# Attention and gated-MLP kernel on one core: wider loads of keys, queries, values and gates, constant rows made on chip, and a new order of all steps

## Chip, cores and metric

One core of a Trainium2 chip runs the whole program. The metric is device time in microseconds (us) for one execution; lower is better. The engines are TensorE (PE; its weight loads appear as PEld), VectorE (DVE), ScalarE (ACT), GpSimd (POOL) and SyncE (SP), each with its own instruction stream. DMA transfers are issued from the streams of SP, ACT or POOL and all run on the same 16 DMA engines.

## What is computed

The reference is an mLSTM attention block followed by a gated MLP. Batch B=4, heads H=8, sequence S=768, head size D=40.

```
for t in range(S):
    m_new = max(f_gate[t] + m, i_gate[t])
    f_stab, i_stab = exp(f_gate[t] + m - m_new), exp(i_gate[t] - m_new)
    C = f_stab * C + i_stab * outer(v[t], k[t])
    n = f_stab * n + i_stab * k[t]
    y[t] = sigmoid(o_gate[t]) * (C @ q[t]) / max(|n . q[t]|, 1)
x = y with the heads side by side                 # (4, 768, 320)
h = relu(x @ w_in); u, v = halves of h            # 512 columns each
v_n = (v - mean) / sqrt(var + 1e-6)               # over the 512 columns
v_s = w_spatial @ v_n + b_spatial                 # over the 768 positions
out = (u * v_s) @ w_out
```

## The kernel before

**Attention** (function attention, from L557). The sequence is cut into chunks of 128 positions, six per batch, 24 in all, named by n; each chunk is two half-chunks of 64. For a chunk TensorE forms the scores of each head (step s, L605), the exponents of the decay matrix as one matrix product of two small tables, AT (positions) and GM (gates) (ex, L608), and in batch 0 also the decay of the queries (ebm, L618). ScalarE takes the exponential (W, L623), VectorE multiplies scores by it (ks, L629), GpSimd decays queries (q, L637) and keys (kt, L648). TensorE makes the state's increment (dc, L659/L661) and the outputs (pv, L702/L703); the state goes from chunk to chunk through the steps d1, c1, d2, c2 (L677 to L690). Then come the denominator (den, L714 to L717, three VectorE instructions), the division and the output gate (xm L720, xg L723), and a transposition (px, L743) that leaves x as a high and a low part (xh, xl).

**MLP.** a_v makes the v half and its normalisation (V, L796 and what follows), b_u the u half and the product with w_spatial (pu L856, pb L862 to L864), c_out the output (L899 to L901). Every operand of these products is split into a high and a low part, so each is three or two matrix products. The weights are split on chip: cvt (L442 to L490) for w_in and w_out with one ScalarE and several VectorE instructions, load_ws (L526 to L544) for w_spatial, whose low part is a VectorE subtraction at L540.

**Gates** (L320 to L431). The scans over 768 positions are cut into three pieces, z0 (128 positions), z1 (256) and z2 (384). z0's rows go straight from SBUF into GM (four small transfers on SP, steps dg, L418) and AT (two on ACT, da, L424). All pieces are also written to scratch arrays in memory (wg L404, wa L408, on the ACT stream; we L411, on SP), and later chunks read their rows from there (gm L584, ra L438; in batch 0 on the ACT stream, in later batches on SP; eb L592 on SP).

**Loads.** QK of a chunk is two transfers on SP of 40 partitions each (L572: partitions 64 to 103 and 0 to 39), from two buffers in turn. RH (values, keys and output gates) is two transfers of 64 partitions (L576), from three buffers in turn; GpSimd clears 32 partitions of each RH buffer once (L314). The constant rows of GM (84 partitions) and AT (68 partitions), two buffers each, come from memory by four transfers issued on GpSimd (L300, L303).

**Order.** The functions only register steps, each with an engine, the buffers that it reads and writes, and a cost. The order in which they are issued is a written-out list of names, ORDER (L98 to L150). The function ordered takes it as it is, and hands out buffer slots in that order; the costs and due times given to add decide nothing here. So every engine, and every DMA-issuing stream, runs its steps in the order of the list: a step that waits holds up all later steps of its stream. The list before begins:

```
half_neg rhz0 ident i sel f warm qk0_0 cgm0 qk0_1 cat0 rh0_0 cgm1 rh0_1 rhz1 wir_ld wi0 wi10_ld wi11_ld m0 rst rh1_0 m1 ksz2 rh1_1 ksz0 fa1 qk1_0 fs1
rhz2 qk1_1 fa0 ksz1 g1 s0 cat1 fs0 gh1 g0 eg1 is0 as0 gh0 gl1 ah0 dg0 gl0 da0 dg1 al0 wg1 m2 dg2 da1 dg3 wg0 eg0 fa2 th0 fs2 wa0 g2 gm1 ex0 is1 ebm0
```

Here qk, rh, cgm and cat are the loads named above; wir_ld, wi10_ld and wi11_ld load 512 KB of w_in each; m, fa, fs, g, is, as are the scans and subtractions of a piece, gh, gl, ah, al their high and low parts.

Of the kernel before, what the change touches and what calls it, by code (L numbers as in the profile page):

```python
# [98 lines left out]
half_neg rhz0 ident i sel f warm qk0_0 cgm0 qk0_1 cat0 rh0_0 cgm1 rh0_1 rhz1 wir_ld wi0 wi10_ld wi11_ld m0 rst rh1_0 m1 ksz2 rh1_1 ksz0 fa1 qk1_0 fs1  # L99
rhz2 qk1_1 fa0 ksz1 g1 s0 cat1 fs0 gh1 g0 eg1 is0 as0 gh0 gl1 ah0 dg0 gl0 da0 dg1 al0 wg1 m2 dg2 da1 dg3 wg0 eg0 fa2 th0 fs2 wa0 g2 gm1 ex0 is1 ebm0  # L100
gh2 rh2_0 W0 gl2 rh2_1 Eb0 as1 ks0_0 ebm1 wir_1 ks0_1 kt0 ah1 wir_2 we1 q0_1 Eb1 dc0 wir_3 wi10_1 c1_0 al1 wir_h0 qk2_0 wi10_2 pv0 qk2_1 is2 wa1 wir_4
wir_h1 den0 d2_0 wir_h2 wi10_3 wi11_1 xm0 as2 wir_h3 wi11_2 ra01 wi11_3 wi10_h0 wi10_4 wi11_h0 wir_s0 q1_0 ah2 wi11_4 gm2 wg2 xg0 q1_1 eg2 wir_5 ex1
rh3_0 th1 rh3_1 wi10_5 s1 W1 al2 wi10_s0 gm3 px0 qk3_0 wir_s1 kt1 wa2 qk3_1 ex2 wi11_5 xh0 we0 xj0 W2 wi11_s0 dc1 th2 wi10_l0 kt2 s2 ra02 wir_l1 ebm2
wi11_l0 Eb2 c2_0 dc2 gm4 xl0 d1_1 th3 xk0 ks1_0 V00 q2_0 ks1_1 c1_1 ks2_0 d2_1 pv1 ks2_1 re00 q2_1 c2_1 sq00 ex3 bsp den1 ebm3 s3 xm1 W3 d1_2 qk5_0
xg1 Eb3 qk5_1 va00 wir_l0 px1 kt3 rh4_0 gm5 rh4_1 c1_2 q3_0 xh1 dc3 ks3_0 xj1 ks3_1 pv2 d2_2 xl1 xk1 ex4 den2 q3_1 ebm4 W4 V01 c2_2 xm2 wi00_ld Eb4
xg2 wi01_ld d1_3 qk4_0 qk4_1 po00 px2 c1_3 re01 rh5_0 pv3 d2_3 nb00 rh5_1 xh2 xj2 ra10 xl2 gm6 th4 kt4 s5 c2_3 sq01 den3 we2 d1_4 xm3 ws00_ld dc4 vh00
# [867 lines left out]
```

## Time and profile before

| | |
|---|---|
| time, median of 3 runs | 421.42 us (419.78 to 424.54) |
| the profiled execution's own time | 424.52 us |
| its span, first to last instruction | 422.7 us |
| PE busy | 369.7 us, 87% of the span |
| DVE, ACT, POOL busy | 250.9, 152.5, 139.8 us |
| mean granted TensorE clock | 0.927 |
| bytes read and written in memory | 30.59 and 4.42 MB |

Starts are in us from the start of the span. In a row of a timeline the first number is the start, the second the length; in a row of waits the numbers are the total, the count and the longest; in a row of stages each engine's busy time stands with its count of instructions in brackets, and the three last columns are the granted TensorE clock, the mean busy share of the DMA engines and the rate in GB/s.

### The profile page before, as it was taken

The numbers are of one execution on the slowest core, as the hardware profiler recorded it, in microseconds if no ns is written. First come the engines' busy times: TensorE is split into PE (matmuls) and PEld (weight loads), VectorE is DVE, ScalarE is ACT, GpSimd is POOL, SyncE is SP. The second block draws the span as 40 slices with busy tenths as digits, with TensorE's granted clock in tenths as the row PEclk, the third lists the DMA queues.
The fourth block names the chain that finished last, engine by engine and source line by source line (L and its number), as shares of the span: only waits on it lengthen the run. The fifth ranks groups of instructions, "written<-read, shape, count | busy, mean of one in ns | idle before, by whom it ended". The sixth has DMA issues, their size and how long they took to land.

```text
span 422.7 us, 9190 instructions
## 1 busy us (share of the span) xinstructions
PE 369.7 (87%) x3654; PEld 335.1 (79%) x3654; DVE 250.9 (59%) x540; ACT 152.5 (36%) x363; POOL 139.8 (33%) x150
## 2 busy tenths in 40 slices
PE   2045996979969999989799989999799999999996
PEld 1023874768869998868699878998699998899995
DVE  6145979867998737569693574335952626434231
ACT  2044268646331205723501521156320408441212
POOL 8044578753350114546530313325440004230000
PEclk9999999677969999989779985999779999999999
DMA  9940569354820505326312073200210100000001
GB/s 166 227 116 12 133 202 223 118 139 118 213 75 18 158 30 143 102 79 154 101 46 73 7 185 92 85 16 24 72 47 2 33 16 2 33 16 2 16 33 47
DMA packets 17262, 35.62 MB, mean 84 GB/s; under 512 B 3960, under 2 KB 9196, under 8 KB 17220
## 3 DMA queue, kind: packets, MB, share of 16 engines
q1 hardware_dynamic: 12556, 29.72, 26.6%
q10 hardware_dynamic: 4136, 4.52, 3.3%
q0 software_dynamic: 528, 0.81, 1.2%
q8 instruction: 29, 0.48, 0.5%
q14 instruction: 13, 0.11, 0.1%
HBM read 30.59 MB, written 4.42 MB: 83 GB/s over the span
## 4 chain that ended last, share of the span: by engine, by line
PE 67%; DVE 14%; DMA 10%; issue 4%; ACT 3%; POOL 1%; SPq 1%; ACTq 0%; DVEq 0%; POOLq 0%
PE pu L856 9%; PE pb L862 8%; PE pb L863 8%; PE pb L864 8%; PE pm L796 7%; PE pv L702 5%; DMA QK<-in_qk 5%; PE s L605 5%; PE pv L703 4%; PE pc L899 3%; PE pc L901 3%; PE pc L900 2%; PE dc L659 2%; DMA RH<-in_vk 2%; DVE KS L629 2%
## 5 line engine op out<-in xcount | busy, mean ns | idle before, releaser
L637 POOL TENSOR_TENSOR KS<-QK,Eb 40x512 f32<-40x512 f32 x44 | 57.5, 1312 | 70.1 <-PE pv L703 32.8
L862 PE MATMUL pb<-wsH,vH 128*128 128x384 f32 x192 | 68.0, 354 | 3.9 <-DVE wo_r L468 3.9
L863 PE MATMUL pb<-wsL,vH 128*128 128x384 f32 x192 | 67.1, 350 | 0.0
L864 PE MATMUL pb<-wsH,vL 128*128 128x384 f32 x192 | 66.9, 349 | 0.0
L873 DVE TENSOR_TENSOR pb<-pb,bsp 128x384 f32<-128x384 f32 x32 | 18.1, 565 | 54.3 <-PE pb L864 54.3
L883 ACT CAST gt<-pb 128x384 fp32r<-128x384 f32 x32 | 15.4, 480 | 76.7 <-DVE pb L876 76.7
L703 PE MATMUL pv<-RH,KS 128*64 128x41 f32 x384 | 37.9, 254 | 5.1 <-DVE KS L629 3.2
L702 PE MATMUL pv<-RH,KS 104*64 104x41 f32 (+1 forms) x384 | 38.0, 253 | 4.7 <-DVE KS L629 3.0
L605 PE MATMUL s<-QK 40*64 40x64 f32 x768 | 34.3, 251 | 8.9 <-DMA QK<-in_qk 8.9
L862 PEld LDWEIGHTS pb<-wsH,vH 128*128 128x128 f32 x192 | 38.1, 198 | 4.4 <-DVE wo_r L468 4.2
L605 PEld LDWEIGHTS s<-QK 40*64 40x64 f32 x768 | 30.6, 162 | 13.5 <-DMA QK<-in_qk 9.2
L812 POOL TENSOR_TENSOR st<-st,half_neg 128x1 f32<-128x1 f32 x24 | 13.4, 560 | 82.0 <-DVE st L809 65.8
L702 PEld LDWEIGHTS pv<-RH,KS 104*64 104x64 f32 (+1 forms) x384 | 31.2, 158 | 10.9 <-POOL st L812 3.3
L836 POOL TENSOR_TENSOR vL<-v,vH 128x512 fp32r<-128x512 f32 x24 | 31.1, 1299 | 23.6 <-ACT vH L818 15.2
L863 PEld LDWEIGHTS pb<-wsL,vH 128*128 128x128 f32 x192 | 38.2, 199 | 0.0
L864 PEld LDWEIGHTS pb<-wsH,vL 128*128 128x128 f32 x192 | 38.0, 198 | 0.0
L703 PEld LDWEIGHTS pv<-RH,KS 128*64 128x64 f32 x384 | 31.2, 159 | 7.7 <-DVE KS L629 2.8
L629 DVE TENSOR_TENSOR KS<-s,W 64x512 f32<-64x512 f32 x48 | 32.9, 686 | 6.9 <-PE s L605 4.3
L648 POOL TENSOR_TENSOR RH<-RH,W 128x320 f32<-128x320 f32 x24 | 18.7, 781 | 49.0 <-ACT W L623 34.9
L856 PE MATMUL pu<-xH,wiH 128*128 128x384 f32 x96 | 33.1, 345 | 0.0
L856 PE MATMUL pu<-xH,wiL 128*128 128x384 f32 x96 | 32.6, 340 | 0.0
L796 PE MATMUL pm<-wiH,xH 128*128 128x512 f32 x72 | 31.5, 437 | 0.0
(117 smaller groups left out, 818.8 us busy)
## 6 DMA issues: line engine op xcount, KB each, us to landing
RH<-in_vk SPq DMA_DIRECT2D x48, 242.0 KB
QK<-in_qk SPq DMA_DIRECT2D x48, 160.0 KB
out<-o ACTq DMA_DIRECT2D x24, 160.0 KB
Eb<-scr_e SPq DMA_DIRECT2D x33, 80.0 KB
ws<-in_w_sp SPq DMA_DIRECT2D x12, 192.0 KB
wi_raw<-in_w_in SPq DMA_DIRECT2D x4, 512.0 KB
wo_raw<-in_w_out SPq DMA_DIRECT2D x4, 320.0 KB
wir_raw<-in_w_rem SPq DMA_DIRECT2D x1, 512.0 KB
```

Source lines behind the costliest of these rows:

```text
L605: self.nc.tensor.matmul(o[64 - p0:128 - p0, h], q[p0:p0 + D, 0, h], q[p0:p0 + D, 1, h], start=True, stop=True)
L629: self.nc.vector.tensor_tensor(out=KS.t[r, e], in0=st()[r], in1=self.T(W)[r], op=ALU.mult)
L637: self.nc.gpsimd.tensor_tensor(out=KS.t[r, e], in0=self.T(QK)[r, 1], in1=self.T(Eb)[r], op=ALU.mult)
L648: self.nc.gpsimd.tensor_tensor(out=kt, in0=kt, in1=self.T(W)[:, :, L - 1:L].broadcast_to([128, H, D]), op=ALU.mult)
L702: self.nc.tensor.matmul(o[0:64, h], ks[0:ke, 0, h], v0[0:ke, h], start=True, stop=True)
L703: self.nc.tensor.matmul(o[64:128, h], ks[:, 1, h], v1[:, h], start=True, stop=True)
L796: self.nc.tensor.matmul(pmt(), l, r, start=i == 0, stop=i == len(terms) - 1)
L836: self.nc.gpsimd.tensor_tensor(out=vl(), in0=vt(), in1=vh().bitcast(F32), op=ALU.subtract)
L856: self.nc.tensor.matmul(put(), w, x, start=i == 0, stop=i == len(terms) - 1)
L862: self.nc.tensor.matmul(pbt(), vH[:, cd], wh[:, s], start=s == 0, stop=False)
L863: self.nc.tensor.matmul(pbt(), vH[:, cd], wl[:, s], start=False, stop=False)
L864: self.nc.tensor.matmul(pbt(), vL[:, cd], wh[:, s], start=False, stop=s == NB - 1)
```

## The change

Keys and queries of a chunk come in one transfer of 112 partitions; the rows between are zeros laid into the input (448 KB in place of two of 160 KB). Values of the second half-chunk, keys and gates come in one transfer of 128 partitions (484 KB, zeros included, which replaces the clearing by GpSimd), values of the first half-chunk in another of 64 partitions (82 KB). Of the constant rows only a few come from memory: a 64 by 64 mask (16 KB), 16 rows for each GM (32 KB) and 4 for each AT (12 KB); the other rows are copied on chip from the mask and from the identity matrix, by ScalarE for the first buffer and GpSimd for the second. In the gates, the additions and subtractions of z1 and z2 that ran on VectorE go to GpSimd, and the scratch writes and the reads of batch 0 go from the ACT stream to SP. The low parts of the first half of w_spatial go from VectorE to GpSimd. In batch 0 the denominator is one ScalarE and two VectorE instructions in place of three on VectorE. The two products of each head in pv change places. ORDER is new throughout. Costs and due times also change in many places, which decides nothing in the program.

```
 ORDER = """
-half_neg rhz0 ident i sel f warm qk0_0 cgm0 qk0_1 cat0 rh0_0 cgm1 rh0_1 rhz1 wir_ld wi0 wi10_ld wi11_ld m0 rst rh1_0 m1 ksz2 rh1_1 ksz0 fa1 qk1_0 fs1
-rhz2 qk1_1 fa0 ksz1 g1 s0 cat1 fs0 gh1 g0 eg1 is0 as0 gh0 gl1 ah0 dg0 gl0 da0 dg1 al0 wg1 m2 dg2 da1 dg3 wg0 eg0 fa2 th0 fs2 wa0 g2 gm1 ex0 is1 ebm0
...
+half_neg rst msk i f atr0 ident ko0 warm gmr1 qk0 ksz1 va_0 gmr0 wir_ld gmc0 wi0 m0 ksz0 atc0 fa0 fs0 sel g0 ksz2 is0 gh0 as0 atr1 th0 dg1 gl0 m1 ah0
+dg0 da0 al0 s0 eg0 dg2 m2 da1 dg3 gmc1 wi11_ld wi10_ld wir_1 qk1 fa1 wir_2 va_1 ko1 fs1 wir_3 ex0 is1 wir_4 wir_h3 ebm0 g1 W0 Eb0 ks0_0 kt0 gh1 ks0_1
+as1 dc0 wi11_1 wir_5 wir_h0 gl1 wa0 wi11_2 wir_h1 q0_1 wg1 s1 wir_h2 c1_0 wi11_3 wi10_1 d2_0 ko2 wi10_2 wi11_h0 fa2 pv0 ah1 c2_0 gm1 th1 wir_s0 al1
+gm2 eg1 qk2 wi10_3 fs2 wa1 wir_s1 wi10_h0 va_2 is2 wi10_4 da_0 th2 ebm1 dp_0 atc1 xm0 xg0 Eb1 wi10_5 px0 ko3 ra01 g2 ebm2 xh0 wg0 xj0 s2 we1 wi10_s0
...
-            return lambda: self.nc.gpsimd.dma_start(out=F(f"GM{j}").t, in_=self.a["gm"])
-            return lambda: self.nc.gpsimd.dma_start(out=F(f"AT{j}").t[0:68], in_=self.a["at"])
+                self.nc.gpsimd.dma_start(out=F(f"GM{j}").t[68:84], in_=self.a["gmr"])
+                self.nc.gpsimd.dma_start(out=F(f"AT{j}").t[64:68], in_=self.a["atr"])
+                eng = self.nc.gpsimd.tensor_copy if j else self.nc.scalar.copy
+                eng(out=F(f"GM{j}").t[0:L].rearrange("p (h t) -> p h t", h=H), in_=F("msk").t.unsqueeze(1).broadcast_to([L, H, L]))
+                eng(out=F(f"AT{j}").t[0:L].rearrange("p (c t) -> p c t", t=L), in_=F("ident").t[0:L, 0:L].unsqueeze(1).broadcast_to([L, S // L, L]))
-            add(f"rhz{j}", "POOL", 0.38, lambda j=j: self.nc.gpsimd.memset(F(f"RH{j}").t[32:64, o:o + VW], 0.0), w=[(F(f"RH{j}"), "zero")], due=1.0 + 6 * j)
...
-                    self.nc.vector.tensor_tensor(out=f[:, lo:hi], in0=f[:, lo:hi], in1=m[:, lo - 1:hi - 1], op=ALU.add)
+                    sub_eng().tensor_tensor(out=f[:, lo:hi], in0=f[:, lo:hi], in1=m[:, lo - 1:hi - 1], op=ALU.add)
-                self.nc.vector.tensor_tensor(out=f[:, s:hi], in0=f[:, s:hi], in1=m[:, s:hi], op=ALU.subtract)
+                sub_eng().tensor_tensor(out=f[:, s:hi], in0=f[:, s:hi], in1=m[:, s:hi], op=ALU.subtract)
...
-                return self.dma("ACT")(
+                return self.dma("SP")(
                     out=self.scr_g[:, k0:k0 + nb].rearrange("p k r t -> p (k r t)"), in_=gpt().bitcast(F32).rearrange("p k w x -> p (k w x)"))
-                return self.dma("ACT")(out=self.scr_a[:, :, c], in_=apt().bitcast(F32))
+                return self.dma("SP")(out=self.scr_a[:, :, c], in_=apt().bitcast(F32))
...
-            self.nc.vector.tensor_tensor(out=F(f"wsL{q}").t[:, c], in0=tt(), in1=F(f"wsH{q}").t[:, c].bitcast(F32), op=ALU.subtract)
+            eng = self.nc.gpsimd if q in WS_POOL else self.nc.vector
+            eng.tensor_tensor(out=F(f"wsL{q}").t[:, c], in0=tt(), in1=F(f"wsH{q}").t[:, c].bitcast(F32), op=ALU.subtract)
...
-                self.nc.sync.dma_start(out=self.T(QK)[p0:p0 + D], in_=self.a["qk"][b, k, e])
-                self.nc.sync.dma_start(out=RH.t[64 * e:64 * e + 64, e * VW:e * VW + VW + 2 * KW], in_=self.a["vk"][b, k, e])
+            self.nc.sync.dma_start(out=self.T(QK)[0:QR], in_=self.a["qk"][b, k])
+            self.nc.sync.dma_start(out=RH.t[:, VW:RW], in_=self.a["ko"][b, k])
+            self.nc.sync.dma_start(out=RH.t[0:64, 0:VW], in_=self.a["v"][b, k])
...
-                self.dma("SP" if b else "ACT")(
+                self.dma("SP")(
                     out=GM.t[64:68].bitcast(F32).rearrange("r (h t) -> r h t", h=H),
...
+                self.nc.tensor.matmul(o[64:128, h], ks[:, 1, h], v1[:, h], start=True, stop=True)
                 self.nc.tensor.matmul(o[0:64, h], ks[0:ke, 0, h], v0[0:ke, h], start=True, stop=True)
-                self.nc.tensor.matmul(o[64:128, h], ks[:, 1, h], v1[:, h], start=True, stop=True)
...
+        if b in DEN_ACT:
+                self.nc.scalar.activation(out=dt_().unsqueeze(2), in_=pvt()[:, :, D:E], func=AF.Abs, scale=2.0)
+                self.nc.vector.tensor_scalar(out=dt_(), in0=dt_(), scalar1=2.0, scalar2=None, op0=ALU.max)
+                self.nc.vector.reciprocal(out=dt_(), in_=dt_())
```

In the new list ko and va_ are the loads of RH, gmr, atr and msk the small loads, gmc and atc the copies on chip, da_ and dp_ the denominator of batch 0.

More of the change, by code (lines that the diff above doesn't have):

```diff
@@ L30 @@
 KE = 84
+QR = 112
 NKS, NRH = 3, 3
@@ L150 @@
+out33 oc34 out34
 """
@@ L297, in consts @@
         add("rst", "POOL", 0.5, rst, w=[F("rst")], due=0.0)
-        def gm(j):
-            return lambda: self.nc.gpsimd.dma_start(out=F(f"GM{j}").t, in_=self.a["gm"])
-        def at(j):
-            return lambda: self.nc.gpsimd.dma_start(out=F(f"AT{j}").t[0:68], in_=self.a["at"])
-        add("cgm0", "POOL", 0.55, gm(0), w=[F("GM0")], size=168, due=0.1)
-        add("cat0", "POOL", 0.55, at(0), w=[F("AT0")], size=204, due=0.2)
+        add("ident", "ACT", 0.4, lambda: self.nc.scalar.dma_start(out=F("ident").t, in_=self.a["ident"]), w=[F("ident")], size=64, due=-0.5)
@@ new lines, in consts, with gmr, atr, gmc @@
+        add("msk", "SP", 0.4, lambda: self.nc.sync.dma_start(out=F("msk").t, in_=self.a["msk"]), w=[F("msk")], size=16, due=0.5)
+        for j in range(2):
+            def gmr(j=j):
+                self.nc.gpsimd.dma_start(out=F(f"GM{j}").t[68:84], in_=self.a["gmr"])
+            def atr(j=j):
+                self.nc.gpsimd.dma_start(out=F(f"AT{j}").t[64:68], in_=self.a["atr"])
+            def gmc(j=j):
+                eng = self.nc.gpsimd.tensor_copy if j else self.nc.scalar.copy
+                eng(out=F(f"GM{j}").t[0:L].rearrange("p (h t) -> p h t", h=H), in_=F("msk").t.unsqueeze(1).broadcast_to([L, H, L]))
+            def atc(j=j):
+                eng = self.nc.gpsimd.tensor_copy if j else self.nc.scalar.copy
+                eng(out=F(f"AT{j}").t[0:L].rearrange("p (c t) -> p c t", t=L), in_=F("ident").t[0:L, 0:L].unsqueeze(1).broadcast_to([L, S // L, L]))
+            add(f"gmr{j}", "POOL", 0.55, gmr, w=[(F(f"GM{j}"), "r")], size=32, due=0.1 + 3 * j)
+            add(f"atr{j}", "POOL", 0.55, atr, w=[(F(f"AT{j}"), "r")], size=12, due=0.2 + 30 * j)
+            add(f"gmc{j}", "POOL" if j else "ACT", 1.3 if j else 0.6, gmc, r=[F("msk")], w=[(F(f"GM{j}"), "c")], due=2.0 + 6 * j, lock=j > 0)
+            add(f"atc{j}", "POOL" if j else "ACT", 1.9 if j else 0.85, atc, r=[F("ident")], w=[(F(f"AT{j}"), "c")], due=2.0 + 30 * j, lock=j > 0)
@@ L583, in ld_g @@
             def ld_g():
-                self.dma("SP" if b else "ACT")(
+                self.dma("SP")(
                     out=GM.t[64:68].bitcast(F32).rearrange("r (h t) -> r h t", h=H),
                     in_=self.scr_g[b * H:(b + 1) * H, k].rearrange("h r t -> r h t"))
-            add(f"gm{n}", "SP" if b else "ACT", 0.35, ld_g, r=[(F("scr_g"), z)], w=[(GM, ("g", r)) for r in range(4)], size=8)
+            add(f"gm{n}", "SP", 0.4, ld_g, r=[(F("scr_g"), z)], w=[(GM, ("g", r)) for r in range(4)], size=8)
         pe = b == 0
@@ L868, in b_u @@
         add(f"pu{name}", "PE", 1.42, pum, r=[xH, xL] + self.wi_parts(0), w=[pu], due=self.moe_due(b, "pu", i), after=gate, hold=[u])
-        add(f"u{name}", "ACT", 0.45, lambda: self.nc.scalar.activation(out=self.T(u), in_=put(), func=AF.Relu), r=[pu], w=[u])
+        add(f"u{name}", "ACT", 0.49, lambda: self.nc.scalar.activation(out=self.T(u), in_=put(), func=AF.Relu), r=[pu], w=[u])
         vs = [x for s in range(NB) for x in self.vn[b, s]]
```

234 lines of the change are left out of this document (117 added, 117 removed).

## Prediction

> **What bounds the kernel now.** I read the stages first (busy time of each engine in a stretch, granted clock, DMA share, GB/s), then the waits of TensorE, then the start row by row. Stage rows, columns PE, PEld, DVE, ACT, POOL, clock, DMA share, GB/s:
>
> ```profile
> 0.00:20.00 20.00, 2.44 (x32) 2.06 (x32) 8.61 (x19) 2.79 (x7) 8.62 (x20) 1.00 0.95 198
> ...
> 0.00:24.70 24.70, 2.44 (x32) 2.08 (x33) 8.61 (x19) 3.54 (x10) 8.62 (x20) 1.00 0.84 179
> 24.70:140.00 115.30, 96.46 (x1088) 81.80 (x1089) 94.46 (x199) 55.61 (x126) 57.52 (x57) 0.90 0.46 123
> 140.00:422.70 282.70, 270.80 (x2536) 251.22 (x2534) 147.83 (x322) 93.34 (x228) 73.61 (x73) 0.93 0.21 60
> ```
>
> There are three stages. In the first 24.7 us TensorE works 2.4 us while the DMA engines are 84% busy. From 24.7 to 140 us (batch 0, and the splitting of the weights) TensorE and VectorE are both busy for more than 80% of the time: 96.5 and 94.5 of 115.3 us. After 140 us TensorE is busy for 270.8 of 282.7 us, so that at most 11.9 us of idle time are to be had there. The waits of TensorE, over the whole span, then those in 60 to 140 us, then those after 140 us:
>
> ```profile
> PE ex L608 <- DMA GM<-gp: 14.8, 1, 14.8
> PE s L605 <- DMA QK<-in_qk: 8.9, 3, 5.0
> ...
> PE pb L862 <- DVE wo_r L468: 3.9, 1, 3.9
> PE pv L702 <- DVE KS L629: 3.0, 1, 3.0
> ...
> PE pv L703 <- DVE KS L629: 2.7, 1, 2.7
> PE px L743 <- DVE x L723: 2.4, 2, 2.0
> ```
>
> The longest wait is the first product ex for GM's gate rows. The start on the streams of SP, VectorE, ScalarE and TensorE, and sizes of the loads (from the list of DMA issues, KB each):
>
> ```profile
> 1.64 0.83 SPq L572 DMA_DIRECT2D QK<-in_qk  x2
> 2.51 1.19 SPq L576 DMA_DIRECT2D RH<-in_vk  x2
> 3.74 0.59 SPq L452 DMA_DIRECT2D wir_raw<-in_w_rem  x1
> 3.85 0.41 DVE L337 TENSOR_TENSOR_SCAN mt<-ft,it 32x128 f32<-32x128 f32 x1 [2.99 <-DMA ft<-in_f_gate]
> 4.38 1.51 SPq L452 DMA_DIRECT2D wi_raw<-in_w_in  x2
> 5.93 1.26 SPq L576 DMA_DIRECT2D RH<-in_vk  x2
> 7.92 3.39 SPq L572 DMA_DIRECT2D QK<-in_qk  x2
> 12.79 10.29 SPq L418 DMA_DIRECT2D GM<-gp  x4
> ...
> 23.46 0.26 ACT L399 ACTIVATE eg<-gc 32x64 f32<-32x64 f32 x1 [15.26 <-DMA scr_g<-gp]
> ...
> 24.71 0.77 PE L608 MATMUL ex<-GM,AT 84*128 84x512 f32 x1 [14.80 <-DMA GM<-gp]
> ```
>
> ```profile
> RH<-in_vk SPq DMA_DIRECT2D x48, 242.0 KB
> QK<-in_qk SPq DMA_DIRECT2D x48, 160.0 KB
> ...
> wi_raw<-in_w_in SPq DMA_DIRECT2D x4, 512.0 KB
> ...
> AT<-in_at POOLq DMA_DIRECT2D x2, 204.0 KB, 8.6
> ...
> GM<-in_gm POOLq DMA_DIRECT2D x2, 168.0 KB, 7.9
> ```
>
> The four small transfers of the gate rows (L418) are issued from 12.79 to 23.08 us, 2.6 us each, behind transfers that had all been issued by 11.3 us: they sit in a backlog. ScalarE, which issues the scratch writes, stands still with them for 15.26 us. The start is thus a matter of the bytes ahead of GM's gate rows, moved at 198 GB/s.
>
> **The start, by bytes.** The new list puts these rows behind fewer bytes. No longer ahead of them: two loads of AT and two of GM (408 + 336 KB), two of w_in (1024), RH and QK of chunk 1 (484 + 320); together 2572 KB. New ahead of them, by their shapes: the mask (16), the rows of GM (64) and AT (24), 128 more for the wider QK of chunk 0, and the 82 of its first values; together 314 KB. Net 2258 KB, or 2.31 MB, less: at 198 GB/s that is 11.7 us, so ex would begin at 13.0 us rather than at 24.71. A check from the other side, the work before the rows are issued: in the first stage VectorE has 8.6 us of work and the new list makes z0's rows before the scans of z1 and z2. Its steps (a scan of 128 columns, two additions, a scan, the cast) take some 2 us from the landing of the gates (the first scan, L337, starts at 3.85 us; 0.2 to 0.4 us each), the four issues at about 0.6 us each, as L452 took, 2.5 us more, and the read of such rows lands 3.5 us after its issue in the row below: 12 us. The two agree, so I take **11.7 us**. Bounds: 12.9 us at the 179 GB/s of the longer stage; 5.1 us if each of the four issues still takes 2.6 us (from 5.8 to 16.1, landing at 19.6).
>
> ```profile
> 24.30 3.50 DMA GM<-scr_g
> ...
> 40.79 0.47 DVE L723 SCALAR_TENSOR_TENSOR x<-RH,pv 128x320 f32<-128x320 f32 x1
> ...
> 41.36 0.76 PE L608 MATMUL ex<-GM,AT 84*128 84x512 f32 x1 [5.23 <-issue]
> ```
>
> Does the rest move forward by as much? Chunk 1 begins (ex at 41.36) when the output gate of chunk 0 (x, L723) has freed its buffer. That chain hangs on the first ex alone: exponential, ks, dc, pv, den, x. In the new list the read of AT's rows for chunk 1 (ra01) stands on SP right behind the load of RH for chunk 3, which waits for the same x; one landing of 3.5 us follows x. But the VectorE steps between pv and x (a string of w_in conversions before) are fewer, so chunk 1 should begin about 11 us earlier as well. The weight loads, now behind the gate rows, have 1 MB to bring: 5 us from 13 us on, before the first V needs them. The gain is kept.
>
> **Work moved between engines.** Rows of the groups by line (mean or minimum/median/maximum in ns):
>
> ```profile
> L540 DVE TENSOR_TENSOR wsL<-ws,wsH x12: 519/556/1630, 82.3 to 113.3; 128x384 fp32r<-128x384 f32 x12
> ...
> L836 POOL TENSOR_TENSOR vL<-v,vH 128x512 fp32r<-128x512 f32 x24 | 31.1, 1299 | 23.6 <-ACT vH L818 15.2 <-ACT v L828 3.6 <-DMA QK<-in_qk 2.3
> ...
> L715 DVE SCALAR_TENSOR_TENSOR den<-pv,den 128x8 f32<-128x8 f32 x24 | 4.0, 167 | 0.8
> ...
> L353 POOL TENSOR_TENSOR it<-it,mt 32x256 f32<-32x256 f32 x1 | 0.8, 814 | 0.1
> ...
> L345 DVE TENSOR_TENSOR ft<-ft,mt 32x256 f32<-32x256 f32 x1 | 0.4, 416 | 0.0
> ```
>
> Six of the twelve subtractions of L540 leave VectorE: 6 x 0.556 = 3.3 us. In batch 0 one den instruction of three goes: 6 x 0.167 = 1.0 us. Together 4.3 us of VectorE in a stage where it is busy 82% and TensorE waits for it 3.9 + 3.0 us in the two longest cases. I take **3 us** of gain; between nothing (TensorE is as busy as VectorE there) and 4.3. GpSimd pays: a subtraction of 512 columns takes it 1.30 us, so one of 384 about 0.97, six 5.8 us; the six gate steps of z1 and z2 cost 0.81 where VectorE took 0.42, some 5 us in all, and the two copies of constant rows about 3 us by the same rate. That is 14 us on an engine busy 57.5 of 115.3 us, hidden as long as q and kt of a chunk don't queue behind it; uncovered, each such step costs its 0.8 to 1 us once. The copies for the first buffers on ScalarE fall into its 15 us of standstill. The clearing of RH that goes, and the swapped pair in pv, I cost at nothing: the first lies in GpSimd's idle time at the start, the second changes no instruction's size.
>
> **Wider loads.** Per chunk the new transfers bring 128 + 82 = 210 KB more, 5.2 MB in all; at 198 GB/s 1.1 us per chunk. After 24.7 us the DMA engines are busy 46% and 21% of the time, so the cost is nothing as long as a load is issued ahead of its use; without that cover it is 1.1 us in each of the first eight chunks, 9 us, and that is the bound. SP issues three transfers per chunk, not four, which frees some 0.4 us of a stream that is not the bound. The Trainium skill (DMA: Bandwidth & Descriptors, "Why a DMA increments its semaphore by 16 and not by 1") says that a transfer is spread over the largest number of engines up to 16 that divides its partitions: 10 for 40, 16 for 112. By that rule two old transfers put 8 rows of 4 KB on the busiest engine and a new one puts 7, so the padding would cost nothing even in a backlog, and the start would gain 0.6 us more than the bytes say; no row here shows the split.
>
> **The steady stages.** After 140 us the instructions of TensorE are the same in number and shape. The rows above show two waits there that hang on the order alone, 2.7 and 2.4 us. I take **2 us** of gain from the new order, between 5.1 and (see the rivals) a loss.
>
> **Sum.** 424.5 (own time of the profiled execution: 422.7 span and 1.8 around it) - 11.7 - 3 - 2 = 407.8 us. The median of the runs is 3.1 us below that execution's time; the same step gives **404.7**, forecast 405 us.
>
> **Rivals.** (1) *The half clock goes too.* The granted clock falls in stretches; three in the second stage, one typical of later:
>
> ```profile
> 73.90:80.70 6.80, 6.26 (x93) 5.11 (x95) 5.49 (x18) 4.11 (x10) 5.19 (x6) 0.64 0.59 182
> 87.60:97.80 10.20, 8.96 (x40) 7.06 (x41) 6.82 (x15) 1.85 (x3) 4.02 (x4) 0.59 0.37 101
> 118.30:125.10 6.80, 3.72 (x12) 3.72 (x13) 6.66 (x14) 1.78 (x5) 5.75 (x5) 0.64 0.19 55
> ...
> 299.20:309.40 10.20, 9.43 (x110) 8.45 (x111) 8.91 (x21) 2.80 (x7) 6.14 (x6) 0.59 0.29 80
> ```
>
> These stretches lie in the stage in which TensorE waits for VectorE. If a denser order removes the first three, at most half of the 6.26 + 8.96 + 3.72 us busy in them is saved, 9.5 us: 398.3, as a median 395. For it: less VectorE work there. Against: later stretches lie where TensorE is busy 96% of the stage, so thin spells come from the small products too. The Trainium skill (TensorE: Matmul & The Clock Gate, "HAM oscillation — how this bites in real kernels") lays the drop to idle gaps of over about 3.4 us; by that rule fewer waits mean fewer stretches, but the stretch at 299 us follows no wait of that length in the rows of waits. (2) *More half clock.* The new order groups attention's small products otherwise and meets two more stretches of 10.2 us like the last row, each costing half of 9.43: 4.7 us. 407.8 + 9.4 = 417.2, as a median 414. (3) *Slower: SP becomes a queue of waits.* The scratch writes and reads of batch 0 now stand on SP among loads that wait for buffers:
>
> ```profile
> SPq L576 <- DVE x L723: 14.6, 2, 12.4
> ```
>
> SP stood 12.4 us before one load of RH. If the reads of GM and AT are held behind such a load once, and then lie open with a landing of 3.5 us in chunks 1, 3, 4 and 5, that is 12.4 + 14.0 = 26.4 us: 434.2, as a median 431. It decides once more than the 16.7 us of gains are held up. For it: a write, its landing and its read follow each other closely on SP in the new list. Against: ScalarE, which carried them, held W and Eb up with them, and no longer does. (4) *The change does not do what it says:* the gate rows are held up by something other than bytes, and the start stays as it is; 421. Against it: the backlog adds up to the issue times above.
>
> **Chances.** Forecast 0.52, (1) 0.20, (2) 0.13, (3) 0.10, (4) 0.05. A measurement tells about 1% (4.2 us) from no change here. Faster by over 1% (under 417.2): nearly all of the forecast, all of (1), two thirds of (2): 0.80; within 1%: the rest of these and (4): 0.10; slower: 0.10. The range goes from 389 (the forecast with the 9.5 us of (1) and the larger bounds of the start and of the later waits, not all of them) to 420 (the start alone, 424.5 - 11.7, with the 9.4 us of (2), less 3.1). It leaves out (3), (4) and a little on the low side.
>
> **What would show it.** Right: ex begins at 12 to 15 us, L418 is issued without a gap of microseconds, ScalarE has no wait of 15 us, chunk 1's ex begins near 30 us, VectorE's busy time falls by 4 to 6 us and GpSimd's rises by some 12, and the stage after 140 us is as long as before. Wrong: ex begins before 15 us but the second stage ends where it did (then VectorE or the loads were the bound all along); or SP's waits before L584 and L438 appear as waits of ex and eb; or the granted clock of the last two stages is lower than 0.90 and 0.93.

## The result, and the profile after

The changed kernel takes 393.12 us (median of 4 runs, 390.08 to 402.0), the kernel before in the same session 422.98 us (median of 4). The ratio is 0.9293 with a 95% interval of 0.9161 to 0.9426. The profiled execution of the changed kernel took 390.08 us, that of the kernel before 424.52: 34.4 us less. The forecast was 16.7 us less between profiles, and 405 us. Medians, here and below, are over all runs, while the ratios leave out slow runs, which lie over 1.5% above the fastest of their kernel, as the one of 402.0 us does.

Busy time of each engine over the span (with its share and the count of instructions), before, then after:

```profile
PE 369.7 (87%) x3654; PEld 335.1 (79%) x3654; DVE 250.9 (59%) x540; ACT 152.5 (36%) x363; POOL 139.8 (33%) x150
```

```profile
PE 353.6 (91%) x3654; PEld 319.0 (82%) x3654; DVE 242.7 (62%) x522; ACT 155.3 (40%) x371; POOL 149.7 (39%) x161
```

TensorE runs the same 3654 instructions in 16.1 us less. That is the first surprise: nothing in the diff makes a product smaller. The span and clock, and the stages of the changed kernel (columns as in the prediction):

```profile
core 0: 388.3 us, clock 0.972
```

```profile
0.00:24.70 24.70, 11.71 (x128) 9.50 (x128) 14.85 (x28) 11.79 (x25) 17.78 (x29) 1.00 0.76 215
24.70:140.00 115.30, 102.37 (x1293) 88.10 (x1292) 97.03 (x204) 55.64 (x135) 64.64 (x64) 0.94 0.55 160
140.00:388.30 248.30, 239.57 (x2243) 221.43 (x2239) 130.80 (x291) 87.83 (x213) 67.24 (x68) 0.98 0.22 66
```

By 140 us TensorE has started 293 more instructions than before (2243 are left, where 2536 were), and the granted clock rose in both later stages, from 0.90 to 0.94 and from 0.93 to 0.98. The start, row by row:

```profile
2.44 0.43 SPq L580 DMA_DIRECT2D QK<-in_qk  x1
5.95 3.70 SPq L426 DMA_DIRECT2D GM<-gp  x4
9.70 1.20 SPq L460 DMA_DIRECT2D wi_raw<-in_w_in  x2
12.29 0.76 PE L620 MATMUL ex<-GM,AT 84*128 84x512 f32 x1 [1.27 <-DMA AT<-ap]
...
31.18 1.29 PE L620 MATMUL ex<-GM,AT 84*128 84x512 f32 x2 [0.78 <-ACT Eb L633]
```

The four transfers of the gate rows go out at 5.95 us, not at 12.79, and take 3.70 us to issue, not 10.29. Two of the three early loads of w_in come behind them. The first ex starts at 12.29 us (24.71 before), and chunk 1's at 31.18 (41.36). TensorE's longest waits after (total, count, longest):

```profile
PE s L617 <- DMA QK<-in_qk: 9.7, 2, 9.0
PE px L765 <- DVE x L735: 7.5, 6, 2.6
PE dc L671 <- POOL RH L660: 5.5, 6, 2.0
PE ex L620 <- DMA AT<-ap: 1.3, 1, 1.3
PE pv L714 <- DVE wi_r L476: 1.1, 1, 1.1
```

The wait of 14.8 us for the gate rows is gone; ex now waits 1.3 us, for the rows of AT. Ahead of it stand the 9.0 us until the first keys and queries are there. What is left behind it are waits of 1 to 3 us, most of them in batch 0, for the output gate and for kt on GpSimd.

The 34.4 us can be split three ways, by span = busy time of TensorE + its idle time up to the first ex + its idle time from there on. The time at half clock is worked out from the mean clock: (1 - clock) x 2 x span, as the clock is 1.00 or 0.50 in the rows below.

| kernel (profiled execution) | span | PE busy | idle up to ex | idle after | at half clock |
|---|---|---|---|---|---|
| before | 422.7 | 369.7 | 22.3 | 30.8 | 61.7 |
| after | 388.3 | 353.6 | 10.3 | 24.3 | 21.7 |
| difference | -34.4 | -16.1 | -12.0 | -6.4 | -40.0 |

So 12 us are the start, 6.4 us are later waits, and 16.1 us are products that run faster while the clock is halved for 40 us less. Experiment 5 gives a price by which the clock explains 12.5 of these 16.1 us. The half clock of the kernel before, two of its stretches:

```profile
75.90:82.70 6.80, 6.80 (x84) 5.52 (x82) 5.53 (x17) 3.91 (x8) 4.33 (x5) 0.50 0.44 130
89.50:99.70 10.20, 10.20 (x42) 8.33 (x42) 5.05 (x12) 3.35 (x8) 2.95 (x3) 0.50 0.28 80
```

(The prediction set these windows some 2 us too early, so its rows show 0.64 and 0.59; set rightly, the clock in them is 0.50 and TensorE busy throughout.)

### The profile page after: what moved, and what is told of

Its sections match the earlier page's. It is cut to its first block, busy times and chain, and to the rows that moved or that the text cites. A ratio compares the mean times of both kernels' runs of the same rounds, so it can differ in the third digit from the quotient of the medians.

```text
span 388.3 us, 9144 instructions
## 1 busy us (share of the span) xinstructions
PE 353.6 (91%) x3654; PEld 319.0 (82%) x3654; DVE 242.7 (62%) x522; ACT 155.3 (40%) x371; POOL 149.7 (39%) x161
## 4 chain that ended last, share of the span: by engine, by line
PE 70%; DVE 11%; ACT 7%; DMA 5%; issue 3%; POOL 2%; POOLq 0%; ACTq 0%; SPq 0%; DVEq 0%
PE pu L878 10%; PE pb L884 9%; PE pb L886 9%; PE pb L885 8%; PE pm L818 8%; PE pv L714 6%; PE s L617 4%; PE pc L921 3%; PE dc L671 3%; PE pc L923 3%; PE pc L922 3%; PE pv L715 3%; ACT pm L825 2%; DMA QK<-in_qk 2%; DVE v L854 1%
## 5 line engine op out<-in xcount | busy, mean ns | idle before, releaser
L885 PE MATMUL pb<-wsL,vH 128*128 128x384 f32 x192 | 64.7, 337 | 0.0
L617 PE MATMUL s<-QK 40*64 40x64 f32 x768 | 31.0, 239 | 10.8 <-DMA QK<-in_qk 9.7
L617 PEld LDWEIGHTS s<-QK 40*64 40x64 f32 x768 | 27.8, 151 | 15.6 <-DMA QK<-in_qk 9.0
L884 PEld LDWEIGHTS pb<-wsH,vH 128*128 128x128 f32 x192 | 36.0, 188 | 2.4 <-ACT vH L840 1.3
L885 PEld LDWEIGHTS pb<-wsL,vH 128*128 128x128 f32 x192 | 36.1, 188 | 0.2
L714 PE MATMUL pv<-RH,KS 128*64 128x41 f32 x384 | 33.5, 237 | 1.1 <-DVE wi_r L476 1.1
L714 PEld LDWEIGHTS pv<-RH,KS 128*64 128x64 f32 x384 | 27.2, 141 | 8.3 <-issue 2.6
L715 PE MATMUL pv<-RH,KS 104*64 104x41 f32 (+1 forms) x384 | 33.4, 236 | 0.0
L891 ACT ACTIVATE u<-pu 128x384 f32<-128x384 f32 x32 | 15.6, 492 | 43.9 <-PE pu L878 43.9
L921 PE MATMUL pc<-woH,gt 128*128 128x320 f32 x96 | 30.3, 315 | 0.9 <-ACT gt L905 0.9
```

Of the source, the lines that this page charges most:

```text
L617: self.nc.tensor.matmul(o[64 - p0:128 - p0, h], q[p0:p0 + D, 0, h], q[p0:p0 + D, 1, h], start=True, stop=True)
L714: self.nc.tensor.matmul(o[64:128, h], ks[:, 1, h], v1[:, h], start=True, stop=True)
L715: self.nc.tensor.matmul(o[0:64, h], ks[0:ke, 0, h], v0[0:ke, h], start=True, stop=True)
L884: self.nc.tensor.matmul(pbt(), vH[:, cd], wh[:, s], start=s == 0, stop=False)
L885: self.nc.tensor.matmul(pbt(), vH[:, cd], wl[:, s], start=False, stop=False)
L921: self.nc.tensor.matmul(pct(), gH[:, c], wh[:, d], start=d == 0, stop=False)
```

## The experiments

Two theories stood against each other. Theory A: the time is gained by the start and by the edits to the code. Theory B: most of it is gained by the new order, and much of that through the clock, which is granted in full when TensorE's array always has enough to do.

### 1. The code edits with the old order

The changed code, with ORDER from before; the names of the new loads and copies stand where their forerunners stood. Against the changed kernel:

```
 ORDER = """
-half_neg rst msk i f atr0 ident ko0 warm gmr1 qk0 ksz1 va_0 gmr0 wir_ld gmc0 wi0 m0 ksz0 atc0 fa0 fs0 sel g0 ksz2 is0 gh0 as0 atr1 th0 dg1 gl0 m1 ah0
+half_neg ident i sel f warm qk0 msk gmr0 gmc0 atr0 atc0 va_0 gmr1 gmc1 ko0 wir_ld wi0 wi10_ld wi11_ld
+m0 rst va_1 m1 ksz2 ko1 ksz0 fa1 qk1 fs1 fa0 ksz1 g1 s0 atr1 atc1 fs0 gh1 g0 eg1
...
```

> All edits of the change, but the steps in the old order (each new step at the place of the one that it replaces). Theory: what the change gained beyond the start comes from the order, through fewer stretches at half clock and fewer waits of TensorE; with the old order the gate rows stand behind the weight loads again, only the constant rows are gone from the start. So 412 to 424 us, granted clock 0.92 to 0.94, first ex at 19 to 23 us. Rival: the edits (wider loads, work moved off VectorE, scratch writes off ScalarE's stream) make the gain; then 395 to 405 us.

Measured: 412.02 us (411.07 to 414.24), ratio 0.9746 [0.9688, 0.9805]. The edits alone bring some 11 of 30 us. Ex and the clock (0.946 over the span) lie just outside what was expected, on the better side.

```profile
18.01 0.76 PE L640 MATMUL ex<-GM,AT 84*128 84x512 f32 x1 [10.47 <-DMA GM<-gp]
```

```profile
140.00:410.70 270.70, 257.57 (x2399) 238.55 (x2397) 141.06 (x313) 91.38 (x223) 72.40 (x72) 0.95 0.21 65
```

Ex starts at 18.0 us: fewer bytes ahead, but the weights still stand ahead of the gate rows. By the split of the table, idle time up to ex is 16.0 us (22.3 before), idle time after it 32.0, and busy time 362.7, with 44.4 us at half clock: so the edits alone lower the half clock too, by 17 us. Which of them does it, no run shows.

### 2. The new order with the old code

The code of before, with the new list; ko and va_ in it are again the two loads of RH, gmr and gmc the load cgm, da_ and dp_ the step den. Against the kernel before:

```
 ORDER = """
-half_neg rhz0 ident i sel f warm qk0_0 cgm0 qk0_1 cat0 rh0_0 cgm1 rh0_1 rhz1 wir_ld wi0 wi10_ld wi11_ld m0 rst rh1_0 m1 ksz2 rh1_1 ksz0 fa1 qk1_0 fs1
+half_neg rst i f cat0 ident rh0_0 rh0_1 warm qk0_0 qk0_1 rhz0 ksz1 rhz1 cgm0 wir_ld wi0 m0 ksz0 fa0
+fs0 sel g0 ksz2 rhz2 is0 gh0 as0 th0 dg1 gl0 m1 ah0 dg0 da0 al0 s0 eg0 dg2 m2
...
```

> The kernel before with the new order alone: narrow loads, constant rows from memory, gates and low parts on VectorE, scratch writes on ScalarE's stream. Theory: most of the gain is here, 393 to 403 us, clock 0.95 to 0.98, first ex at 13 to 17 us (372 KB of constant rows more ahead of the gate rows). Rival: 408 to 420 us.

Measured: 402.81 us, ratio 0.9508 [0.9437, 0.9579], some 21 us. With the 11 of experiment 1 that makes 32, and the whole change brings 30: the two halves nearly add up, and two thirds are the order.

```profile
15.02 0.76 PE L628 MATMUL ex<-GM,AT 84*128 84x512 f32 x1 [1.93 <-DMA GM<-gp]
```

```profile
140.00:401.30 261.30, 252.25 (x2405) 232.74 (x2403) 140.79 (x312) 90.82 (x220) 70.43 (x71) 0.98 0.20 59
```

After 140 us the clock is 0.98, as in the whole change, with not one edit to the code. By the split, idle time up to ex is 12.6 us and after it 28.3, and busy time is 360.5, with 36.1 us at half clock over the span: of 21.4 us less span, 9.7 are the start, 9.2 are busy time and 2.5 are later waits.

### 3. The start alone

In the kernel before, eight loads (two of w_in, chunk 1's, the second GM and AT) are moved behind the gate rows; nothing else.

```
-half_neg rhz0 ident i sel f warm qk0_0 cgm0 qk0_1 cat0 rh0_0 cgm1 rh0_1 rhz1 wir_ld wi0 wi10_ld wi11_ld m0 rst rh1_0 m1 ksz2 rh1_1 ksz0 fa1 qk1_0 fs1
+half_neg rhz0 ident i sel f warm qk0_0 cgm0 qk0_1 cat0 rh0_0 rh0_1 rhz1 wir_ld wi0 m0 rst m1 ksz2
...
+dg1 al0 wg1 m2 dg2 da1 dg3 wi10_ld wi11_ld rh1_0 rh1_1 qk1_0 qk1_1 cgm1 cat1 wg0 eg0 fa2 th0 fs2
```

> The kernel before; eight loads (two of w_in, two of RH and two of QK of chunk 1, the second GM and AT) moved behind the four transfers of the gate rows, nothing else. By bytes 2200 KB less ahead of the gate rows, 11.4 us at 198 GB/s: first ex at 13 to 15 us, time 409 to 415 us, clock as before, 0.92 to 0.94. Rival: the earlier start moves everything after it into better places too, 400 us or less; or the second stage takes the gain back, 419 us or more.

Measured: 418.68 us, ratio 0.9885 [0.9846, 0.9925]; 4.9 us gained. The start of ex (13 to 15 us) and the time (409 to 415) miss what was expected; the clock, 0.926, stays as it was.

```profile
8.28 4.17 SPq L438 DMA_DIRECT2D GM<-gp  x4
16.61 0.76 PE L628 MATMUL ex<-GM,AT 84*128 84x512 f32 x1 [7.15 <-DMA GM<-gp]
```

```profile
PE s L625 <- DMA QK<-in_qk: 7.6, 3, 5.6
PE ex L628 <- DMA GM<-gp: 7.2, 1, 7.2
PE ex L628 <- DVE x L743: 5.2, 1, 5.2
PE eb L638 <- DMA GM<-scr_g: 4.8, 1, 4.8
```

Ex starts 8.1 us earlier, but the span is only 4.8 us shorter. By the same split as above, idle time after the first ex grows from 30.8 to 33.6 us and busy time from 369.7 to 370.1: 3.2 us are given back. One row that shows where is eb's wait for GM's rows from scratch, 4.8 us; in the kernel before it was 2.0:

```profile
PE eb L618 <- DMA GM<-scr_g: 2.0, 1, 2.0
```

Here the earlier start is kept only in part: as eb's row shows, not all that follows is ready as much earlier.

### 4. Dense fillers in the kernel before

Theory B says that work on the array keeps the clock up. 54 products of 128 x 512, whose results are overwritten, are added in batches 1 to 3 of the kernel before, one of them ahead of a chunk's scores and two ahead of its pv; this adds work that the reference doesn't need.

```
+            if b:
+                for _ in range(2):
+                    self.nc.tensor.matmul(self.T(pv), F("wiH").t[:, 1, 0:128], F("wiH").t[:, 1, 0:DH], start=True, stop=True)
```

> The kernel before with needless work: in batches 1 to 3 each chunk's scores begin with one dense product (128 rows, 128 columns, 512 moved) and each pv with two, overwritten by the real products; 54 products of about 0.22 us, 12 us of TensorE work added. Theory: the clock halves after some 3.4 us that hold small products only, whether TensorE is idle or not; the fillers keep such spells from forming after 140 us, so clock 0.95 or more and a time of 410 to 424 us in spite of the added work. Rival: idle gaps halve the clock; the fillers change nothing there, clock 0.92 to 0.94 and 430 to 435 us.

Measured: 426.5 us, ratio 1.007 [1.0025, 1.0114]. That is neither the 410 to 424 us of the theory nor the 430 to 435 of its rival; the clock, 0.940 to 0.958 in ten runs, is above the 0.919 to 0.943 of the kernel before.

```profile
140.00:423.60 283.60, 276.17 (x2579) 251.51 (x2577) 147.09 (x322) 93.08 (x227) 73.87 (x73) 0.97 0.21 60
```

After 140 us the clock is 0.97 instead of 0.93: (1 - 0.97) x 2 x 283.6 = 17 us at half clock, not the 37.5 that the four stretches of before add up to there (at 185.1, 205.6, 249.9 and 301.1 us). The fillers cost some 12 us: by two rows of this trace a product of 320 columns starts 0.15 us after the one ahead,

```profile
290.06 0.31 PE L906 MATMUL pc<-woL,gt 128*128 128x320 f32 x1
290.21 0.30 PE L907 MATMUL pc<-woH,gt 128*128 128x320 f32 x1
```

so that one of 512 takes some 0.23 us, and 54 of them 12 us. Yet the kernel is only 2.9 us longer. By the split, busy time grew by 7.6 us (377.3), not by 12, and idle time after the first ex fell by 7.4 (23.4): by this the clock pays for some 5 us, and the rest is paid by idle time, in which fillers can run. So added work raises the clock, but this run can't tell more work on the array from less idle time.

### 5. The changed kernel again

> The changed kernel once more, to compare the next three with on the same chip: 390 to 396 us, clock 0.95 to 0.98.

Measured: 394.86 us, ratio 0.9274 [0.9205, 0.9343], beside the next three on one chip. Its runs and those of the first measurement are one program at different clocks, which gives a price for the half clock. Of seven runs, those at 0.965 to 0.974 (27 to 20 us at half clock) took 390.1 to 393.6 us, those at 0.951 and 0.952 (38 us) 395.1 to 397.4 us: on average 14.7 us more at half clock go with 4.6 us more time, a third. By that, 40 us less are worth 12.5 us, the greater part of the 16.1 us by which TensorE's busy time fell.

### 6. Narrow loads of keys and queries

```
-            self.nc.sync.dma_start(out=self.T(QK)[0:QR], in_=self.a["qk"][b, k])
+            self.nc.sync.dma_start(out=self.T(QK)[64:64 + D], in_=self.a["qk"][b, k][64:64 + D])
+            self.nc.sync.dma_start(out=self.T(QK)[0:D], in_=self.a["qk"][b, k][0:D])
```

> The changed kernel with keys and queries again in two transfers of 40 partitions. Theory that the edits' share of the gain comes from other edits (work off VectorE, scratch writes on SP, constant rows): no difference that can be measured, within 2 us of the changed kernel; by bytes the start gains 128 KB, 0.7 us. Rival, that the wider load removes waits for QK: 3 us or more slower, and longer waits of the scores for QK.

Measured: 395.55 us, ratio 0.9281 [0.9213, 0.9349]. No difference to experiment 5: one transfer of 112 partitions in place of two of 40 is worth nothing that can be measured. The padding of keys and queries costs nothing either; memory reads rose and are hidden (the page of after, and its DMA share of 0.55 and 0.22 above):

```profile
HBM read 35.10 MB, written 4.42 MB: 102 GB/s over the span
```

### 7. Moved work back on VectorE

```
-WS_POOL = (0,)
-DEN_ACT = (0,)
+WS_POOL = ()
+DEN_ACT = ()
-                    sub_eng().tensor_tensor(out=f[:, lo:hi], ...
+                    self.nc.vector.tensor_tensor(out=f[:, lo:hi], ...
```

> The changed kernel with VectorE doing its old work again: six low parts of w_spatial, the gate steps of z1 and z2, three instructions per denominator in batch 0. 4.3 us of VectorE plus 2.9 us of gate steps come back. Theory: 3 to 6 us slower, in the stage up to 140 us. Rival, that TensorE is the bound there: within 1 us.

Measured: 396.77 us, ratio 0.9318 [0.9247, 0.939]: 1.9 us above experiment 5, within both intervals, and between the 3 to 6 of the theory and the 1 of its rival. The work did move: VectorE is busy 246.5 us here and 242.7 in the changed kernel, GpSimd 139.1 and 149.7. The time hardly follows.

### 8. Scratch transfers on ScalarE's stream

```
-                return self.dma("SP")(
+                return self.dma("ACT")(
```

(at the writes wg and wa, and at the reads ra and gm of batch 0)

> The changed kernel with the scratch writes and the reads of batch 0 on ScalarE's stream again. ScalarE then waits for landings (about 3.5 us each, in front of the five reads of GM and two of AT): theory 4 to 10 us slower, with waits of ScalarE for scratch rows. Rival, that the queue does not matter once the backlog at the start is gone: within 2 us.

Measured: 394.29 us, ratio 0.9262 [0.9204, 0.9321]. No difference; the 4 to 10 us that the theory expected did not come. In the changed kernel it doesn't matter which stream issues the scratch transfers; that the shorter backlog is the reason was not tested.

### 9. Constant rows from memory

GM's and AT's constant rows come whole from memory again, in the changed order; the copies on chip are left out.

```
-                self.nc.gpsimd.dma_start(out=F(f"GM{j}").t[68:84], in_=self.a["gmr"])
+                self.nc.gpsimd.dma_start(out=F(f"GM{j}").t, in_=self.a["gm"])
-                eng(out=F(f"GM{j}").t[0:L].rearrange(...), in_=F("msk").t...)
+                pass
```

> The changed kernel with the constant rows of GM and AT from memory again (four transfers at the places of the small ones, nothing copied on chip). 744 KB in place of 120 KB ahead of the gate rows: by bytes 3.2 us later, first ex at 15 to 16 us, time 396 to 400 us. Rival, that the start's backlog is no longer the bound: first ex within 1 us of 12.3, no difference.

Measured: 397.46 us, ratio 0.9435 [0.9383, 0.9488], against 0.9274 in experiment 5 (on another chip) and 0.9293 in the first measurement: 6 to 7 us, with intervals that overlap in the second case.

```profile
12.44 2.92 SPq L424 DMA_DIRECT2D GM<-gp  x4
16.66 0.77 PE L618 MATMUL ex<-GM,AT 84*128 84x512 f32 x1 [5.16 <-DMA GM<-gp]
```

The gate rows are issued at 12.44 us and ex starts at 16.66, 4.4 us later than in the changed kernel, where 3.2 were expected by the bytes. Of the edits tried one by one (experiments 6 to 9) this is the only one that counts.

### 10. Small fillers in the kernel before

A finer theory said that only dense products hold the clock up. As a control, 216 products of the scores' own kind (40 rows, 64 columns) are added in batches 1 to 3; they are overwritten and not needed.

```
+            for h in range(6 if b else 0):
+                for e, p0 in ((0, 64), (1, 0)):
+                    self.nc.tensor.matmul(o[64 - p0:128 - p0, h], q[p0:p0 + D, 0, h], q[p0:p0 + D, 1, h], start=True, stop=True)
```

> The control for the dense fillers: the kernel before, with 12 of the 16 products of the scores made twice in each chunk of batches 1 to 3, which adds the same 0.7 us of TensorE work per chunk, 12 us in all, in small products. Theory: small products do not hold the clock, so clock 0.92 to 0.93, at least 35 us at half clock after 140 us, and 432 to 438 us. Rival, that any added work of TensorE holds the clock: clock 0.945 or more and 423 to 430 us.

Measured: 422.65 us, ratio 1.0023 [0.9977, 1.0068].

```profile
140.00:418.90 278.90, 269.25 (x2896) 250.95 (x2894) 148.28 (x322) 93.12 (x228) 73.72 (x73) 0.98 0.22 61
```

```profile
352.18 0.91 PE L605 MATMUL s<-QK 40*64 40x64 f32 x24
352.93 0.93 PE L608 MATMUL s<-QK 40*64 40x64 f32 x26
```

The fillers of a chunk (first row; the second is the chunk's own scores, 0.75 us later) take 0.75 us, in 18 chunks 13.5 us. The kernel's median is 1.1 us longer, which can't be told from nothing, and the profiled half clock after 140 us fell from 37.5 to 10.2 us; idle time after the first ex fell too, by 3.6 us. The mean clock is 0.936 to 0.959 in ten runs, and 0.919 to 0.943 in those of the kernel before. So the finer theory fell: small products that start close together hold the clock up too.

What, then, lies ahead of the stretches of half clock? One answer is the outputs pv of a batch's first chunk. Before, just ahead of a stretch of half clock, then in it, then pv alone in the first window:

```profile
178.00:185.10 7.10, 6.02 (x116) 4.93 (x113) 6.58 (x14) 1.76 (x5) 3.21 (x4) 1.00 0.32 95
185.10:188.50 3.40, 3.40 (x9) 2.65 (x9) 2.02 (x6) 0.60 (x1) 1.10 (x2) 0.50 0.15 54
```

```profile
178.00:185.10 7.10, 3.94 (x32) 3.03 (x32) 0.01 (x1) 1.00 0.32 95
```

TensorE is counted busy for 6.02 of 7.1 us at full clock, and the clock is halved right behind. 3.94 us of it are the 32 instructions of one pv. The changed kernel shows it without any idle time (TensorE alone; 3.87 us are again such a pv, and from 86.7 to 90.1 us the clock is 0.50):

```profile
79.60:86.70 7.10, 7.10 (x72) 1.00 0.00 0
```

But this is one answer, not the only one. Such a pv starts at 29.8, 88.3, 180.0 and 254.6 us before, and only the stretch at 185.1 begins right behind one (that at 89.5 begins 1.2 us into one). In the changed kernel, too, half clock follows one of the four. In the 7.1 us ahead of the other six TensorE is idle for 1.6 to 3.0 us, as here ahead of the other three after 140 us (TensorE alone):

```profile
198.50:205.60 7.10, 4.81 (x84) 1.00 0.32 89
242.80:249.90 7.10, 5.52 (x97) 1.00 0.91 212
294.00:301.10 7.10, 4.44 (x91) 1.00 0.30 95
```

In an ordinary chunk the 32 instructions of pv take a quarter of that time. First such a chunk of the changed kernel, then an ordinary one:

```profile
173.26 0.31 PE L714 MATMUL pv<-RH,KS 128*64 128x41 f32 x2
173.50 0.31 PE L715 MATMUL pv<-RH,KS 64*64 64x41 f32 x2
173.73 0.31 PE L714 MATMUL pv<-RH,KS 128*64 128x41 f32 x2
...
135.99 0.23 PE L714 MATMUL pv<-RH,KS 128*64 128x41 f32 x1
136.00 0.23 PE L715 MATMUL pv<-RH,KS 104*64 104x41 f32 x1
136.05 0.23 PE L714 MATMUL pv<-RH,KS 128*64 128x41 f32 x1
136.05 0.23 PE L715 MATMUL pv<-RH,KS 104*64 104x41 f32 x1
```

A batch's first chunk has nothing to add from a chunk before it, so one product of each head has 64 rows instead of 104. A product is two instructions here. Where 64 and 128 rows alternate, a new product starts only every 0.237 us; where 104 and 128 alternate, an instruction of each size starts together with one of the other, a pair every 0.058 us, so that two products take 0.116 us. The Trainium skill (TensorEngine Tiling (Array Packing), "Key Properties") says that a change of the tiling mode, not merely of the tile, drains TensorE; these rows fit that, and no row shows the drain itself. Two kernels follow from it.

### 11. pv of first chunks grouped by size

In the changed kernel, in the first chunk of each batch, all products of 128 rows and then all of 64.

```
-            for h in range(H):
+            for e in ((1,), (0,)) if k == 0 else ((1, 0),):
+                for h in range(H):
```

> The changed kernel; in the first chunk of each batch pv makes its eight products of 128 rows first and then its eight of 64 rows, in place of one after the other in turn. In the traces pv takes 3.64 us in these four chunks and 0.9 us in the others, whose rows are 128 and 104. Theory: it is the turns between 64 and 128 rows that cost; 1 to 2 us per chunk then, 6 to 10 us in all, 384 to 391 us. Rival, that products of 64 rows are slow in themselves: 3 us or more per chunk still, no difference.

Measured: 385.02 us (379.4 to 385.74), ratio 0.9083 [0.8997, 0.9169]: by the ratios some 8 us less than the changed kernel.

```profile
171.67 1.13 PE L716 MATMUL pv<-RH,KS 128*64 128x41 f32 x16
172.72 1.06 PE L718 MATMUL pv<-RH,KS 64*64 64x41 f32 x15
```

The group takes some 2.0 us in place of 3.6 to 3.9. That is still twice the time of an ordinary pv: the instructions follow each other 0.058 us apart, and none starts together with another.

### 12. pv of first chunks with 104 rows

In the changed kernel, first chunks use 104 rows like all others; the 40 state rows are set to zero by GpSimd (four small memsets for RH, one for KS). The same outputs are computed.

```
-            ke = 64 if k == 0 else 64 + D
+            ke = 64 + D
+            add(f"cz{n}", "POOL", 0.4, lambda: self.nc.gpsimd.memset(RH.t[hi, 0:VW], 0.0), w=[(RH, "c0")])
```

> The changed kernel; in the first chunk of each batch pv has 104 rows like the others, with the state's rows cleared by one GpSimd memset per batch (and the decayed queries of the first chunk of all by one more). Theory: 0.9 us per chunk in place of 3.64, 11 us less in all where TensorE is the bound, and one thin spell less per batch: 380 to 388 us. Rival, that the first pv of a batch waits for something else: no difference.

Measured: 378.69 us (377.35 to 379.24), ratio 0.9001 [0.8965, 0.9037]. This is better than the 380 to 388 us expected, and beats both kernels: 43 us under the one before on this chip.

```profile
165.78 0.23 PE L739 MATMUL pv<-RH,KS 128*64 128x41 f32 x1
165.78 0.23 PE L740 MATMUL pv<-RH,KS 104*64 104x41 f32 x1
```

```profile
PE 339.4 (90%) x3654; PEld 308.3 (82%) x3654; DVE 241.7 (64%) x522; ACT 154.8 (41%) x371; POOL 150.7 (40%) x166
```

```profile
core 0: 376.7 us, clock 0.981
```

More rows cost no time here: the pairs start together, pv takes 0.9 us, and TensorE's busy time falls by another 14.2 us. Four groups from 3.64 to 0.9 us are 11 us; the rest goes with the half clock, 14 us where it was 21.7. Three stretches of it are left, at 52.1, 65.7 and 328.5 us, none of them behind the first pv of a batch.

## Why the prediction was right, and where it was not

The direction, the range (389 to 420) and the largest term held; the size did not. The result, 393, lies nearest to rival (1), 395.

- **The start, 11.7 us.** Right: ex came 12.4 us earlier, and the rows went out at 5.95 us, where the reckoning by steps had 5.8. That the reckoning by bytes fits to within 1 us is in part luck: by the same 198 GB/s experiment 3 should have gained 11.4 us and gained 8.1, and experiment 9 should have lost 3.2 and lost 4.4. "The gain is kept" held with the new order. In the old order (experiment 3) it was not: 4.9 of 8.1 us remained. The claim rested on chunk 1's chain alone, which came out right in the changed kernel (chunk 1's ex came 10.2 us earlier, though by its row it waits for Eb on ScalarE and not for x), but it named no condition.
- **Work moved between engines, 3 us.** Not borne out. VectorE's busy time fell by 8.2 us, more than the 4.3 counted (the sum charged the gate steps to GpSimd but did not take them off VectorE), and GpSimd's rose by 9.9, not 14; but moving it back costs 1.9 us, which can't be told from nothing (experiment 7). The lower bound, nothing, was the better choice.
- **Wider loads, nothing.** Right for keys and queries, by experiment 6, on both sides: neither cost nor gain. The wider load of RH wasn't tried alone.
- **The constant rows.** Rightly counted among the bytes; experiment 9 prices them at 6 to 7 us, more than the 4.4 us of ex.
- **The steady stages, 2 us.** This is the step that failed. "After 140 us the instructions of TensorE are the same in number and shape" is true, and the conclusion that little is to be had there was wrong, since their speed is not the same: the stage was to stay as long as before, and the part of the span behind 140 us fell from 282.7 to 248.3 us, of which part is the earlier start. Seven stretches of half clock lay in the trace; the prediction charged them to no term, and allowed for three of them, before 140 us, only as a rival of chance 0.20. The change lowered half clock from 61.7 to 21.7 us over the whole program, and busy time fell by 16.1 us with it; the order alone lowers it to 36.1 and the edits alone to 44.4 (experiments 1 and 2). Idle time after the first ex fell by 6.4 us, where the terms of VectorE and of the order had 3 + 2: that much was right in sum, by luck as far as the 3 of VectorE go.
- **Rival (1)** had the right term with some 60% of its size (9.5 of 16.1 us), because it was confined to the stretches before 140 us. Its argument against itself, "thin spells come from the small products too", was half of the clue: one of the seven stretches follows a group of small products, and the other six have waits ahead of them as well. Another order lowers the half clock (experiment 2), and so do needless products (4 and 10). The rule that was weighed there, of idle gaps (TensorE: Matmul & The Clock Gate, "HAM oscillation — how this bites in real kernels", in the Trainium skill), doesn't cover the window of 178 to 185 us, where 1.1 us of 7.1 are idle and the clock falls all the same, and still less that of the changed kernel from 79.6 to 86.7 us, where nothing is idle.
- **Rival (2)**, more half clock, and **rival (3)**, SP as a queue of waits, did not come; in experiment 8 the stream that issues the scratch transfers changes nothing. **Rival (4)** fell with the rows at 5.95 us.

Shown: that order alone brings 21 us and a clock of 0.98 after 140 us; that extra work of TensorE lowers the time at half clock; that the clock can fall with TensorE counted busy throughout; that the alternating sizes in pv cost some 8 us (experiment 11), and that 104 rows in their place bring some 12 (experiment 12). Only argued: that the new order works through the clock by setting dense products between thin ones. What exactly the clock answers to, and at which level, stays open; the clock of one program varies from run to run (0.951 to 0.974). Fillers in the changed kernel, a grouped pv in the kernel before, and the swapped pair in pv alone weren't tried.

## What to carry to other kernels

When TensorE is busy for nine tenths of the span, ask at which clock and how densely its array works, not only where it waits: time at half clock is a term of the sum like any other. Look for groups whose instructions start one after another where a like group overlaps; here, zero rows that make two sizes alike were worth more than any part of the change tried alone but its order. And ask of an earlier start whether the inputs of the next chunks come earlier with it: in experiment 3 they didn't, and 3.2 of 8.1 us were given back.

## What the runs showed of the hardware

- The granted clock fell from 1.00 to 0.50 at 185.1 us behind 7.1 us in which TensorE was busy for 6.0: it halves without a long wait. Two thirds of that busy time was one group whose products start 0.237 us apart. In the changed kernel it fell at 86.7 us behind 7.1 us in which TensorE was counted busy throughout, 3.87 of them such a group. Ahead of the other six stretches of the kernel before, 1.6 to 3.0 of 7.1 us were idle.
- 12 to 13.5 us of needless products made the kernel 1.1 to 2.9 us longer: half clock after 140 us fell from 37.5 us to 17 and 10.2, and idle time after the first ex by 7.4 and 3.6.
- Products (of two instructions each) of 64 and 128 rows in turn start 0.237 us apart, and 16 of them take 3.64 us. Of 104 and 128 rows in turn, 16 take 0.9 us. Grouped by size, 16 take 2.0 us.
- The issue of the same four small transfers took 10.29 us before, behind the loads of the start, 4.17 in experiment 3 and 3.70 after, both with over 2 MB less ahead of them, and 2.92 in experiment 9, with 624 KB more ahead than after: it doesn't follow the bytes ahead alone.
